# First batch of a fused attention and MLP kernel: last-chunk scores of chunks 2 to 4 computed once and transposed by DMA, diagonals of chunks 3 and 4 folded

## The chip, the cores and the metric

The kernel runs on one core of a Trainium2 chip. The metric is the device time of one execution in microseconds (us), as a median over several runs; lower is better. The core has a matrix engine (TensorE, PE in the profile), a vector engine (VectorE, DVE), a scalar engine with activation functions (ScalarE, ACT), a general engine (GpSimd, POOL) and a queue engine that issues transfers here (SyncE, SP). 16 DMA engines carry the transfers that SyncE, ScalarE and GpSimd issue.

## What is computed

There are 8 batches of 3008 rows. For each batch, with `z` of width 64, `v` and `u` of width 256:

```python
scores = (1.0 / S) * np.matmul(z, z.transpose(0, 2, 1))
attn = np.maximum(scores, 0.0) ** 2
x = u * np.matmul(attn, v)
```

and then, over all 24064 rows, a gated MLP with 2048 inner columns:

```python
h = x @ w_in
g = h * (1.0 / (1.0 + np.exp(-1.702 * h)))
out = g @ w_out
```

The score matrix is `z` times its own transpose, so it is symmetric: the block of keys a and queries b is the transpose of the block of keys b and queries a. The squared relu keeps that.

## The kernel before

**Tiles.** The 3008 rows of a batch are 24 blocks of 128 (`NJ`), the last one half full, or 6 chunks of 512 (`NCH`), the last one 448 wide. A *unit* `(i, jp)` is the score of the query chunk `i` against the key blocks `2*jp` and `2*jp + 1`, so a chunk of queries has 12 units. `scores` (lines 207 to 222) computes a unit with two matmuls of contraction 64, which sit in the two halves of TensorE's rows, into a PSUM tile `sc`; there are two such tiles. `square` (lines 224 to 254) then runs a relu on ScalarE (`rl`, line 231) and a square on VectorE (`a`, line 245). A unit with keys right of its own chunk is also transposed by a DMA, issued from SyncE (line 251), into half of a tile `tt`; the other chunk of the pair reads that tile in place of a unit of its own.

**Use.** `attend(b, i)` (lines 273 to 329) multiplies `v` by the squared scores for the queries of chunk `i`: one *step* for each key block `j`, in the order that the list `js` gives. `weights` (lines 256 to 270) says for a step where its scores lie: in a unit of chunk `i`, in a transposed tile, or, in later batches, in units of other chunks whose queries are already the last chunk. For chunks 0 and 1 of the first batch a step is one matmul over all 128 rows, in other cases two that share the array by halves of its rows.

**Two rules for the last chunk and the diagonal.** In batches 1 to 7, for chunks 0 to 4, the units `(i, 10)` and `(i, 11)` (last-chunk keys against queries of chunk `i`) are computed the other way round: as keys of chunk `i` against queries of chunk 5 (`turned`, line 212). Chunk 5 then reads them as they are, and chunk `i` reads their transposes, so chunk 5 has only two units of its own, `(5, 10)` and `(5, 11)`. Also in these batches the second of the two diagonal units is *folded* (line 204): only half of it is computed, and the other half comes by a DMA transpose (`ad`, line 238) from the first diagonal unit. In batch 0 neither is done: chunk 5 computes all its 12 units, and chunks 0 to 4 have plain units for its keys.

**Order of the work.** The order on each engine is the order in which the program is written, by hand. `pieces(b, i)` lists a chunk's units, `fill(b)` puts them in one queue, and the tables `SCHED0` (batch 0, lines 570 to 577) and `SCHED` say at which step of which chunk how many units are taken from the queue (`take`, line 581). So the scores of a chunk are computed in the steps of the chunk before it or its own. The loads of `u` come from GpSimd at steps given by `LOAD0`: that for chunk 3 at step 28 of chunk 1, that for chunk 4 at step 28 of chunk 2; each follows the turn of an earlier `u` tile on VectorE (line 194), whose buffer it takes. While batch 0 runs chunk 5, the first groups of the MLP (`up_group`) are set between its steps. SyncE's queue holds, in batch 0, the loads of `z` and `v`, then the transposes in the order of their units, with one load of `u` among them.

In batch 0 before, units are taken like this: all of chunk 0 and `(1, 2)`, `(1, 3)` by the end of chunk 0; in chunk 1 two units at each of the steps 0, 8, 15, 22, 30 and 38, which are the rest of chunk 1 and `(2, 4)` to `(2, 7)`; in chunk 2 `(2, 8)` to `(2, 11)` at steps 0, 3, 7 and 11, then the six of chunk 3; in chunk 3 the four of chunk 4 and two of chunk 5; in chunk 4 the other ten of chunk 5.

Of the kernel before, what the change touches and what calls it, by code (L numbers as in the profile page):

```python
# [15 lines left out]
def kernel(  # L16
# [20 lines left out]
    NJ = (S + P - 1) // P  # L37
# [3 lines left out]
    NCH = (S + CH - 1) // CH  # L41
    CB = CH // P
    NU = NJ // 2
# [38 lines left out]
    def post(last):  # L82

        sig = pool.nop()  # L84
        for m in last:
            tc.add_manual_dep(sig.ins, m.ins.name, SYNC, reason="row tiles of one bank")
        return sig

    def behind(sig, m):
        tc.add_manual_dep(m.ins, sig.ins.name, SYNC, reason="row tiles of one bank")  # L90
# [86 lines left out]
    def width(i):  # L177
        return CH if i < NCH - 1 else LAST
# [23 lines left out]


    def folded(b, i):
        return b > 0 and i < NCH - 1

    def scores(b, group):
        scs = []
        zt = ZT[b]
        for i, jp in group:  # L210
            sc = ps2.tile([P, 2, CH], F32, name="sc", tag="ps2")
            turned = b > 0 and i < NCH - 1 and jp >= NU - 2
            kp, qi = (2 * i + jp - (NU - 2), NCH - 1) if turned else (jp, i)
            m = CB // 2 if folded(b, i) and jp == 2 * i + 1 else CB
            for r in range(2):
                h = slice(r * DQK, (r + 1) * DQK)
                pe.matmul(  # L217
                    sc[:, r, :m * P], zt[h, 2 * kp + r, :], zt[h, (qi + 1) * CB - m:(qi + 1) * CB, :],
                    start=True, stop=True,
                )  # L220
            scs.append(sc)
        return [lambda u_=u_, sc=sc: square(b, *u_, sc) for u_, sc in zip(group, scs)]

    def square(b, i, jp, sc):
        rl = pw.tile([P, 2, CH], F16, name="rl", tag="rl", bufs=3)
        if folded(b, i) and jp == 2 * i + 1:
            rh = rl[:, :, :CH // 2]
            act.activation(rh, sc[:, :, :CH // 2], AF.Relu, scale=csc)
            dve.tensor_tensor(unit[b, i, jp][:, 1], rh, rh, ALU.mult)
            return  # L230
        act.activation(rl, sc, AF.Relu, scale=csc)  # L231
        if folded(b, i) and jp == 2 * i:
            a = pa.tile([P, CB, 2, P], F16, name="a", tag="a", bufs=21)
            unit[b, i, jp] = a
            r4 = rl.rearrange("p r (q c) -> p r q c", q=CB)
            dve.tensor_tensor(a.rearrange("p q r c -> p r q c"), r4, r4, ALU.mult)
            unit[b, i, jp + 1] = pa.tile([P, 2, 2, CH // 2], F16, name="ad", tag="a", bufs=21)
            sp.dma_start_transpose(
                unit[b, i, jp + 1][:, 0].rearrange("p g (r c) -> p (g r) c", c=P),
                a[:, CB // 2:].rearrange("p q r c -> p (q r c)"),  # L240
            )
            return
        a = pa.tile([P, 2, CH], F16, name="a", tag="a", bufs=21)
        unit[b, i, jp] = a
        dve.tensor_tensor(a, rl, rl, ALU.mult)  # L245
        cj = jp // 2
        if cj > i and (b or cj < NCH - 1):
            if (b, i, cj) not in TT:
                TT[b, i, cj] = pa.tile([P, CB, CB, P], F16, name="tt", tag="tt", bufs=14)
            k0 = 2 * (jp % 2)  # L250
            sp.dma_start_transpose(
                TT[b, i, cj][:, k0:k0 + 2].rearrange("p r g c -> p (r g) c"),
                a.rearrange("p r c -> p (r c)"),
            )

    def weights(b, i, j):

        cj, g = divmod(j, CB)
        n = NCH - 1
        if b == 0 and n in (i, cj):  # L260
            return unit[b, i, j // 2][:, j % 2, :width(i)]
        if i < n and cj == n:
            return TT[b, i, n][:, :, g, :]
        if folded(b, i) and cj == i:
            return unit[b, i, j // 2][:, :, g % 2, :]
        if i == n and cj < n:
            return unit[b, cj, NU - 2 + g // 2][:, g % 2, :LAST]
        if cj >= i:
            return unit[b, i, j // 2][:, j % 2, :width(i)]
        return TT[b, cj, i][:, :, g, :]  # L270


    def attend(b, i, both=False):


        n = width(i)
        js, cs = list(range(NJ - 1)), range(2)
        own = i * CB
        if b == 0 and i in (3, 4):
            js = js[own:-CB + 1] + js[:own] + js[-CB + 1:]  # L280
        elif b and i == NCH - 3:
            js = js[own:own + 2] + js[own + CB:-CB + 1] + js[:own] + js[own + 2:own + CB] + js[-CB + 1:]
        elif b and i < NCH - 2:
            js = js[own:own + 2] + js[own + CB:-CB + 1] + js[own + 2:own + CB] + js[:own] + js[-CB + 1:]
        half = [(0, TOP, NJ - 1), (1, LOW, NJ - 1)]
        if both:
            order = [[(c, FULL, j)] for j in js[:-CB] for c in cs] + [[(c, FULL, j)] for c in cs for j in js[-CB:]]
            order.insert(-CB, half)
        elif i == NCH - 1:
            order = [half] + [[(c, FULL, j)] for c in cs for j in js]  # L290
        else:
            order = [[(0, TOP, j), (1, LOW, j)] for j in js] + [half] + [[(1, TOP, j), (0, LOW, j)] for j in js]
        flat = [(k, m) for k, ms in enumerate(order) for m in ms]
        first = {c: next(m for m in flat if m[1][0] == c) for c in cs}
        final = {c: [m for m in flat if m[1][0] == c][-1] for c in cs}
        acc, turn = {}, NJ if order[-1][0][1] != FULL else -1

        def step(k):
            done = []
            for m in order[k]:  # L300
                c, h, j = m
                if (k, m) == first[c]:
                    acc[c] = ps1.tile([P, CH], F32, name="o", tag="ps1")
                ins = pe.matmul(  # L304
                    acc[c][:, :n], V16[b][h, j, c, :], weights(b, i, j)[h],
                    start=(k, m) == first[c], stop=(k, m) == final[c],
                )
                if k == turn:
                    behind(acc["sig"], ins)
                done.append(ins)  # L310
            if k == turn - 1:
                acc["sig"] = post(done)
            for c in cs:
                if k == final[c][0]:
                    gate(c)

        def gate(c):
            ut = UT[b, i][:, c].rearrange("p q t -> p (q t)")
            x = XT[b, i]
            if i < NCH - 1 or b % 2:  # L320
                dve.tensor_tensor(x[:, c, :n], acc[c][:, :n], ut[:, :n], ALU.mult)  # L321
            else:
                dve.tensor_tensor(x[:, c, :LFULL], acc[c][:, :LFULL], ut[:, :LFULL], ALU.mult)
                dve.tensor_tensor(XT[b + 1, i][:, c, LAST:], acc[c][:, LFULL:n], ut[:, LFULL:n], ALU.mult)

        XT[b, i] = XT.get((b, i)) or pa.tile([P, NCC, CH], F16, name="xt", tag="xt", bufs=6)
        if i == NCH - 1 and b % 2 == 0:
            XT[b + 1, i] = pa.tile([P, NCC, CH], F16, name="xo", tag="xo")
        return [lambda k=k: step(k) for k in range(len(order))]
# [202 lines left out]

    def pieces(b, i):

        lst = [(i, jp) for jp in range(2 * i if b or i < NCH - 1 else 0, NU)]
        if i == NCH - 1 or b == 0:
            return lst
        k = max(len(lst) - 6, 2)
        return lst[:k] + lst[-2:] + lst[k:-2]

    def split(lst, sizes):
        out_, k = [], 0
        for n in sizes:
            out_.append(lst[k:k + n])
            k += n
        assert k == len(lst)
        return out_

    TAIL = {1: {n: 1 for n in (3, 12, 44, 54)}, 2: {n: 1 for n in (4, 25, 34, 43)}}
    SCHED = {
# [16 lines left out]
    FIRST_ZT = {2: 2, 7: 3, 13: 4, 21: NCH - 1}  # L569
    SCHED0 = {  # L570
        0: {0: 1, 6: 2, 14: 2, 22: 2, 30: 2, 38: 2},
        1: {0: 2, 8: 2, 15: 2, 22: 2, 30: 2, 38: 2},
        2: {n: 1 for n in (0, 3, 7, 11, 30, 34, 38, 42)} | {NJ: 2},
        3: {n: 1 for n in (4, 9, 14, 19)} | {NJ: 2},
        4: {n: 1 for n in (0, 4, 8, 12, 16, 20, 31, 36)} | {NJ: 2},
        5: {},
    }

# [2 lines left out]
    def take(b, n):  # L581
        for post_ in scores(b, [queue.pop(0) for _ in range(n)]):
            post_()

    def fill(b):
        assert not queue
        queue.extend(u_ for i in range(NCH) for u_ in pieces(b, i))
# [20 lines left out]
    for b in range(B):  # L608
        nup = NCH * NFG
        sched, turn, load = (SCHED, TURN, LOAD) if b else (SCHED0, TURN0, LOAD0)  # L610
# [29 lines left out]
        for q in range(head, nup):  # L640
            if more and q in (head + 14, head + 20):
                k = int(q == head + 20)
# [46 lines left out]
```

## Time and profile before

| What | Value |
| --- | --- |
| median of 8 runs | 1206.49 us (1204.51 to 1209.34) |
| profiled execution | 1206.58 us, its span 1204.7 us |
| TensorE busy | 1191.9 us, 99% of the span |
| VectorE busy | 830.4 us, 69% |
| ScalarE busy | 770.3 us, 64% |
| attention of batch 0, chunks 1 to 4 | about 28 to 78 us of the span |
| transposes (tt) in batch 0 | 20 of 230 |

In the profile an engine's line shows its busy time, its share of the span and its instructions. A group is a line of the kernel with an engine, an operation and tiles (output<-input); then come its count, its busy time, the mean time of one in ns, and how long the engine stood idle before it and for whom. `sc` are scores, `rl` and `a` the relu and the square, `tt` the transposed tiles, `ad` a folded diagonal, `o` the attention output. SPq is SyncE's queue.

### The profile page before, as it was taken

The page shows a single profiled execution, that of the slowest core. Times are in us where ns is not written, and L with a number is a line of the kernel's source. Part 1 is how long each engine was busy: PE and PEld are TensorE (multiplying, and loading weights), DVE is VectorE, ACT ScalarE, POOL GpSimd, SP SyncE. Part 2 cuts the span into 40 slices and gives each one's busy share as a digit, 9 for nine tenths or more (in the row PEclk, how much of TensorE's full clock was granted, in tenths as well). Part 3 has the DMA queues.
Part 4 walks back from the last instruction along what each step waited for, and adds up shares of the span by engine and source line. Part 5 has one row for each costly group of instructions (what it writes and reads, how often), then busy time and mean ns, then how long its engine had stood idle before and what let it go on. Part 6 is the DMA issues. An engine that isn't in the chain of part 4 may idle for free.

```text
span 1204.7 us, 28259 instructions
## 1 busy us (share of the span) xinstructions
PE 1191.9 (99%) x11785; PEld 715.3 (59%) x11785; DVE 830.4 (69%) x1277; ACT 770.3 (64%) x903; POOL 307.1 (25%) x363
## 2 busy tenths in 40 slices
PE   8999999999999999999999999999999999999998
PEld 2446765467644675446765468554775547844577
DVE  6669955597546976469654696648966489564886
ACT  6777684576844768367683666736677376772764
POOL 4144300452004520044200451015510134101000
PEclk9999999999999999999999999999999999999999
DMA  9966389562994639854399443974459754496012
GB/s 231 163 107 125 122 157 161 91 153 74 171 161 87 150 93 169 156 82 137 94 187 144 80 137 98 193 132 77 137 120 189 126 84 149 113 182 115 1 37 71
DMA packets 366592, 152.33 MB, mean 126 GB/s; under 512 B 313312, under 2 KB 358496, under 8 KB 366464
## 3 DMA queue, kind: packets, MB, share of 16 engines
q1 hardware_dynamic: 330320, 114.08, 48.0%
q0 software_dynamic: 35456, 35.86, 14.9%
q8 instruction: 92, 1.51, 0.5%
q10 hardware_dynamic: 688, 0.59, 0.2%
q14 instruction: 36, 0.29, 0.1%
HBM read 60.29 MB, written 24.64 MB: 71 GB/s over the span
## 4 chain that ended last, share of the span: by engine, by line
PE 95%; DVE 2%; DMA 2%; ACT 1%; issue 0%; SPq 0%; ACTq 0%
PE o L304 38%; PE hg L345 26%; PE st L445 17%; PE yp L511 7%; PE sc L217 6%; DMA tt<-a 1%; DVE a L245 1%; ACT rl L231 0%; DVE gt L354 0%; DMA zf<-in_z_dram 0%; DVE zst L123 0%; ACT gf L353 0%; DVE s L416 0%; DVE s L418 0%; PE zp L129 0%
## 5 line engine op out<-in xcount | busy, mean ns | idle before, releaser
L353 ACT ACTIVATE gf<-hg 128x1024 f32<-128x1024 f32 (+1 forms) x384 | 385.8, 1007 | 165.0 <-PE hg L345 137.8
L231 ACT ACTIVATE rl<-sc 128x1024 f16<-128x1024 f32 x311 | 308.1, 1026 | 209.4 <-PE sc L217 207.4
L304 PEld LDWEIGHTS <-V 64*128 64x128 f16 (+1 forms) x4052 | 233.9, 94 | 252.6 <-issue 11.4
L345 PE MATMUL hg<-xt,W 128*128 128x512 f16 (+1 forms) x1408 | 354.5, 374 | 0.1
L354 DVE TENSOR_SCALAR gt<-gf 128x1024 f16<-128x1024 f32 (+1 forms) x384 | 275.5, 718 | 88.9 <-ACT gf L353 85.0
L245 DVE TENSOR_TENSOR a<-rl 128x1024 f16<-128x1024 f16 x276 | 192.0, 697 | 185.2 <-ACT rl L231 180.3
L304 PE MATMUL o<-a,V 64*128 64x512 f16 (+2 forms) x2010 | 317.2, 372 | 0.0
L187 POOL DMA_DIRECT2D uq<-in_u_dram x188 | 129.5, 696 | 511.1 <-PE sc L217 343.8
L304 PE MATMUL o<-tt,V 64*128 64x512 f16 (+1 forms) x1762 | 215.2, 376 | 2.2 <-DMA tt<-a 2.2
L345 PEld LDWEIGHTS <-W 128*128 128x128 f16 x1536 | 141.2, 98 | 117.4 <-issue 0.3
L445 PEld LDWEIGHTS <-gt 128*128 128x128 f16 x2176 | 132.4, 98 | 29.8 <-issue 1.1
L217 PE MATMUL sc<-ZT 64*128 64x512 f16 (+1 forms) x692 | 121.4, 367 | 1.8 <-DVE ZT L137 0.8
L445 PEld LDWEIGHTS <-s 128*128 128x128 f16 x1632 | 99.2, 98 | 20.7
L172 POOL CAST V<-vst 128x512 f16<-128x512 f32 x96 | 90.5, 981 | 64.8 <-DMA vst<-in_v_dram 51.0
L511 PE MATMUL yp<-W,gt 64*128 64x256 f16 x1664 | 103.9, 269 | 0.0
L511 PEld LDWEIGHTS <-gt 64*128 64x128 f16 x1664 | 80.4, 94 | 19.2 <-POOLq L84 4.1
L321 DVE TENSOR_TENSOR xt<-o,ut 128x512 f16<-128x512 f32 x80 | 51.5, 685 | 38.1 <-PE o L304 38.1
L445 PE MATMUL st<-WT,gt 128*128 128x128 f16 x1088 | 71.8, 219 | 0.9 <-ACT uP L455 0.9
L445 PE MATMUL st<-W,gt 128*128 128x128 f16 x1088 | 71.7, 219 | 0.0
L445 PE MATMUL st<-WT,s 128*128 128x128 f16 x1088 | 71.5, 219 | 0.0
L455 ACT ACTIVATE uP<-st 128x256 f32<-128x256 f32 x102 | 39.1, 383 | 39.6 <-DVE y L461 35.0
L217 PEld LDWEIGHTS <-ZT 64*128 64x128 f16 x692 | 37.5, 94 | 37.8 <-issue 7.1
(47 smaller groups left out, 628.6 us busy)
## 6 DMA issues: line engine op xcount, KB each, us to landing
vst<-in_v_dram SPq DMA_DIRECT2D x39, 512.0 KB, 5.1
uq<-in_u_dram POOLq DMA_DIRECT2D x156, 128.0 KB, 3.4
out_dram<-y SPq DMA_DIRECT2D x33, 512.0 KB, 3.8
tt<-a SPq DMA_TRANSPOSE x230, 3.5
uq<-in_u_dram POOLq DMA_DIRECT2D x32, 112.0 KB, 2.9
out_dram<-y POOLq DMA_DIRECT2D x7, 512.0 KB, 5.1
vst<-in_v_dram SPq DMA_DIRECT2D x8, 384.0 KB, 4.8
out_dram<-y POOLq DMA_DIRECT2D x7, 384.0 KB, 5.1
```

Source lines behind the costliest of these rows:

```text
L172: pool.tensor_copy(V16[b][:, n0:n0 + VB, k, :].rearrange("p n (q c) -> p n q c", c=QW), vst.rearrange("p n (q k c) -> p n q k c", k=NCC, c ...
L187: eng.dma_start(uq[k * QW:(k + 1) * QW, :n // QW].rearrange("t q k c -> t q (k c)"), src[:, :, cs])
L217: pe.matmul(sc[:, r, :m * P], zt[h, 2 * kp + r, :], zt[h, (qi + 1) * CB - m:(qi + 1) * CB, :], start=True, stop=True,)
L231: act.activation(rl, sc, AF.Relu, scale=csc)
L245: dve.tensor_tensor(a, rl, rl, ALU.mult)
L304: ins = pe.matmul(acc[c][:, :n], V16[b][h, j, c, :], weights(b, i, j)[h], start=(k, m) == first[c], stop=(k, m) == final[c],)
L321: dve.tensor_tensor(x[:, c, :n], acc[c][:, :n], ut[:, :n], ALU.mult)
L345: pe.matmul(hg[:, e, :n], W1[:, c, ff * P:(ff + 1) * P], XT[b, i][:, c, :n], start=(c == 0), stop=(c == NCC - 1),)
L353: act.activation(gf[:, :, :n], hg[:, :, :n], AF.Gelu_apprx_sigmoid, scale=1.0 / FSC)
L354: dve.tensor_scalar(g, gf[:, :, :n], FSC, None, ALU.mult)
L445: pe.matmul(bank[:, m, :], lhs()[:, f, m, :], right[:, ff, :], start=name in ("P1", "P2", "P5") and m == 0 and ff == 0, stop=ff == NFF // ...
L511: ins = pe.matmul(yp[s // per][:, s % per, :], GT[b, k, ff // CB][h, ff % CB, s * P:(s + 1) * P], W2[h, ff, :], start=new, stop=n == last[ ...
```

## The change

In batch 0, chunks 2, 3 and 4 follow the rule of the later batches for the last chunk (`turned` is now a function), and chunks 3 and 4 fold their second diagonal unit. Chunk 5 of batch 0 keeps the units `(5, 0)` to `(5, 3)`, for the keys of chunks 0 and 1, and `(5, 10)`, `(5, 11)`; six units are no longer computed. Six units more are transposed by DMA, and two half diagonals. In a chunk whose last-chunk units are turned, these two are now taken first. `SCHED0` takes units at other steps: chunk 1 at steps 0, 7, 14, 21, 28 and 34 (two each) and 40 (one), which now end with `(2, 10)` and `(2, 11)` at step 28, `(2, 4)`, `(2, 5)` at 34 and `(2, 6)` at 40; chunk 2 at 0, 4, 8, 24 (two), 28, 33, 38 and 43. The order of steps changes too: chunk 2 reads blocks 0 to 11, then 20 to 22, then 12 to 19; chunk 3 takes the order that the later batches have; chunk 4 takes the natural order.

```diff
     def folded(b, i):
-        return b > 0 and i < NCH - 1
+
+        return i < NCH - 1 and (b > 0 or i > 2)
+
+    def turned(b, i):
+
+        return i < NCH - 1 and (b > 0 or i > 1)
...
-            turned = b > 0 and i < NCH - 1 and jp >= NU - 2
-            kp, qi = (2 * i + jp - (NU - 2), NCH - 1) if turned else (jp, i)
+            turn = turned(b, i) and jp >= NU - 2
+            kp, qi = (2 * i + jp - (NU - 2), NCH - 1) if turn else (jp, i)
...
-        if cj > i and (b or cj < NCH - 1):
+        if cj > i and (turned(b, i) or cj < NCH - 1):
...
-        if b == 0 and n in (i, cj):
+        if n in (i, cj) and not turned(b, min(i, cj)):
             return unit[b, i, j // 2][:, j % 2, :width(i)]
...
-        if b == 0 and i in (3, 4):
-            js = js[own:-CB + 1] + js[:own] + js[-CB + 1:]
-        elif b and i == NCH - 3:
+        if b == 0 and i == 2:
+            js = js[:own + CB] + js[-CB + 1:] + js[own + CB:-CB + 1]
+        elif i == NCH - 3:
             js = js[own:own + 2] + js[own + CB:-CB + 1] + js[:own] + js[own + 2:own + CB] + js[-CB + 1:]
...
-        lst = [(i, jp) for jp in range(2 * i if b or i < NCH - 1 else 0, NU)]
-        if i == NCH - 1 or b == 0:
-            return lst
+        lst = [(i, jp) for jp in range(2 * i, NU)]
+        if i == NCH - 1:
+            return [(i, jp) for jp in range(2 * i) if not turned(b, jp // 2)] + lst
+        if b == 0:
+            return lst[-2:] + lst[:-2] if turned(b, i) else lst
...
-        1: {0: 2, 8: 2, 15: 2, 22: 2, 30: 2, 38: 2},
-        2: {n: 1 for n in (0, 3, 7, 11, 30, 34, 38, 42)} | {NJ: 2},
-        3: {n: 1 for n in (4, 9, 14, 19)} | {NJ: 2},
-        4: {n: 1 for n in (0, 4, 8, 12, 16, 20, 31, 36)} | {NJ: 2},
+        1: {0: 2, 7: 2, 14: 2, 21: 2, 28: 2, 34: 2, 40: 1},
+        2: {n: 1 for n in (0, 4, 8, 28, 33, 38, 43)} | {NJ: 2},
+        3: {n: 1 for n in (4, 9, 14)} | {NJ: 2},
+        4: {n: 1 for n in (4, 12, 34)} | {NJ: 2},
         5: {},
```

An unused helper, `split`, is also removed.

More of the change, by code (lines that the diff above doesn't have):

```diff
@@ L533, in pieces @@
     def pieces(b, i):
-        lst = [(i, jp) for jp in range(2 * i if b or i < NCH - 1 else 0, NU)]
-        if i == NCH - 1 or b == 0:
-            return lst
+        lst = [(i, jp) for jp in range(2 * i, NU)]
[3 more added lines that the diff above has]
+            return lst[-2:] + lst[:-2] if turned(b, i) else lst
         k = max(len(lst) - 6, 2)
         return lst[:k] + lst[-2:] + lst[k:-2]
[L541 to L547, printed above, removed]
     TAIL = {1: {n: 1 for n in (3, 12, 44, 54)}, 2: {n: 1 for n in (4, 25, 34, 43)}}
```

## The prediction

> **What bounds the kernel now.** I read the page first, then the chain that ended last, then TensorE's order in the first 80 us, then the DMA queues of that stretch.
>
> ```profile
> PE 1191.9 (99%) x11785; PEld 715.3 (59%) x11785; DVE 830.4 (69%) x1277; ACT 770.3 (64%) x903; POOL 307.1 (25%) x363
> ...
> PE 95%; DVE 2%; DMA 2%; ACT 1%; issue 0%; SPq 0%; ACTq 0%
> ...
> L304 PE MATMUL o<-tt,V 64*128 64x512 f16 (+1 forms) x1762 | 215.2, 376 | 2.2 <-DMA tt<-a 2.2
> ```
>
> The chain is TensorE for 95%. So a matmul that goes is worth its full slot, and a wait of TensorE costs its full length: it has no slack in which to make it up. The last line shows the one wait of attention matmuls that the whole run knows: 2.2 us for transposed blocks (tt) that had not landed. The change puts more such blocks into the first batch, so I ask when they land.
>
> TensorE around the border of chunks 1 and 2 of the first batch, in order of time (start, length, line, tiles):
>
> ```profile
> 36.84 0.60 PE L217 MATMUL sc<-ZT 64*128 64x512 f16 x4
> 37.37 1.90 PE L304 MATMUL o<-a,V 128*128 128x512 f16 x8
> 39.21 0.60 PE L217 MATMUL sc<-ZT 64*128 64x512 f16 x4
> 39.74 2.33 PE L304 MATMUL o<-a,V 128*128 128x512 f16 x10
> 42.01 0.39 PE L217 MATMUL sc<-ZT 64*128 64x512 f16 x2
> 42.23 0.81 PE L304 MATMUL o<-tt,V 64*128 64x512 f16 x6
> ```
>
> These give the slots. A unit of scores or a pair of row tiles takes 0.216 us (42.01 to 42.23). In chunk 1, which works with full 128-row tiles, a visit to scores costs 0.21 us more than its matmuls: 36.84 to 39.21 is 2.37 us for 2 units and 8 matmuls, ten slots, 2.16 us.
>
> The SyncE queue in the same stretch, where the transposes are issued, and two of them alone; then, for each of those two, the time from issue to landing; then VectorE's squares of units (1,8) and (1,9), and GpSimd:
>
> ```profile
> 31.78 19.03 SPq L251 DMA_TRANSPOSE tt<-a  x9
> ...
> 42.53 2.83 SPq L251 DMA_TRANSPOSE tt<-a  x1
> ...
> 45.45 1.39 SPq L251 DMA_TRANSPOSE tt<-a  x1
> ```
> ```profile
> DMA to landing us min/median/max: 7.3/7.3/7.3
> ...
> DMA to landing us min/median/max: 5.1/5.1/5.1
> ```
> ```profile
> 33.75 0.69 DVE L245 TENSOR_TENSOR a<-rl 128x1024 f16<-128x1024 f16 x1 [0.55 <-ACT rl L231]
> 34.66 0.69 DVE L245 TENSOR_TENSOR a<-rl 128x1024 f16<-128x1024 f16 x1 [0.22 <-ACT rl L231]
> ...
> 39.01 2.57 POOL L187 DMA_DIRECT2D uq<-in_u_dram  x4 [9.34 <-DVE ut L194]
> ```
>
> Nine transposes stand back to back over 19.0 us, 2.1 us each, though the shortest issue in this queue is 1.2 us. Their sources wait for the queue: (1,8) and (1,9) are squared by 34.4 and 35.4, but are issued at 39.2 and 40.6. The queue is behind by 5 us, and while the fourth u load of GpSimd (39.0 on) shares the DMA engines, a transpose takes 5 to 7 us to land. Before, nobody minds: the two issued at 42.5 and 45.4 are (2,6) and (2,7), whose block is first read in chunk 3, at about 58 us.
>
> **The change part by part.**
>
> *Score work that goes.* Chunk 5 drops 6 of its 12 units: 6 x 0.216 = 1.30 us of TensorE. The second diagonal unit of chunks 3 and 4 is half as wide: 2 x 0.108 = 0.22 us. Sum 1.52 us. ScalarE and VectorE lose 6 x 1.03 and 6 x 0.69 us and two halves; they end nothing here (64% and 69% busy), so that is worth nothing by itself.
>
> *Score work that moves.* Chunk 1 now has seven visits to scores (steps 0, 7, 14, 21, 28, 34, 40) with 13 units, not six with 12. The unit is only moved; the visit adds 0.21. Visits stand 6 or 7 steps apart, 1.94 to 2.15 us, and ScalarE needs 1.94 us for a pair of units with two score buffers, so a later unit waits for its buffer: I take 0.4 us in all (0.1 to 0.7; the one visit before that comes 7 steps after another loses 0.05).
>
> *The two transposes in front.* Units (2,10) and (2,11) are now scored at step 28 of chunk 1. Before, the visit at step 30 began at 36.84 with as many units behind it, so this one begins near 36.4. ScalarE is done with the pair by 38.8, VectorE, with the turn of u ahead of it, by about 39.8. On SyncE the same 12 transposes of chunks 0 and 1 and the u load stand ahead of them as before, so they are issued in the very places that (2,6) and (2,7) had: 42.5 and 45.4. With those rows' times they land at 42.53 + 7.3 = 49.8 and 45.45 + 5.1 = 50.6.
>
> *Who waits.* In chunk 2 the new order reads blocks 0 to 11, and then 20 to 22, which is the transposed block of these two units; both halves are needed at once. Chunk 2 begins at 42.01 + 0.22 + 0.21 + 0.4 = 42.8. Twelve steps and three units (steps 0, 4, 8) are 15 x 0.216 = 3.24 us, so the block is wanted at 46.1 and is there at 50.6: TensorE stands for 4.5 us. Queued behind on TensorE are 35 steps of chunk 2 and the visits to scores of chunk 3, so ScalarE, VectorE and the later transposes start later too; nothing runs ahead meanwhile. Bounds: if the two land as the quickest row of this stretch (issue 1.3, landing 3.2 us), 42.5 + 1.3 + 3.2 = 47.0, a stand of 0.9 us; with the longest landing among the first batch's twenty (8.6 us; their median is 5.9), 54.0, 7.9 us. I take 4.5, because the rows are those of the same queue places behind the same loads.
>
> *The clock after the stand.* The only long gap of TensorE before is that at 13 us. By stretches (length; busy time of PE, PEld, DVE, ACT, POOL; granted clock; DMA):
>
> ```profile
> 13.30:15.30 2.00, 0.00 (x0) 0.00 (x0) 2.00 (x4) 0.39 (x1) 2.00 (x3) 1.00 1.20 279
> 15.40:18.70 3.30, 3.07 (x12) 1.01 (x13) 1.80 (x5) 1.46 (x2) 3.30 (x7) 0.50 1.14 223
> ```
>
> After a gap of 2.4 us the clock is halved for some 3.3 us. A gap of 4.5 us will do the same. How much of the slow stretch falls inside the gap is open: none costs 1.7 us, all of it 0. I take 1.2, as part of it should lie in so long a gap.
>
> The Trainium skill ("TensorE: Matmul & The Clock Gate", section "Why this matters for your kernels") allows gaps up to about 3 us before the clock falls; here 2.4 us were enough, so the row decides that even a shorter stand would cost clock. By that page's window of 3.4 us at half rate the term would be 1.7 and the sum 0.5 us higher.
>
> *The other transposes.* Six more come: the pairs (3,10),(3,11) and (4,10),(4,11) and two folded diagonals. The pair of chunk 4 has most of a chunk, 12 us, of time. In chunk 3 the folded diagonal is read after 18 steps and three visits, 4.5 us into the chunk; its score stands at step 28 of chunk 2, 19 steps and some units earlier, about 9.5 us before its use. Square and score take 2.4 us, the transpose 2.5 (median of ad) to 6.5 us with two others ahead and a u load beside it: between 2 us early and 1.5 us late. I take 0.2. A folded square costs the same as a plain one (0.692 against 0.697 us in the next batch).
>
> The Trainium skill ("DMA: Bandwidth & Descriptors", section "Latency and other measured facts") gives 261 GB/s for a DMA transpose, an estimate of 1.0 us for one of these 256 KB. Behind the transpose issued at 40.55, which takes 6.9 us to land, the pair would by that be there at 49.5, and the sum 1.1 us lower; the rows of this stretch, where u loads share the engines, say 50.6.
>
> *Sum.* -1.52 + 0.21 + 0.4 + 4.5 + 1.2 + 0.2 = +5.0 us. The profiled execution took 1206.58 us (span 1204.7), practically the median of 1206.49, so the forecast is 1211.5 us. From the second batch on, order and loads are as before; I carry no term for them.
>
> **The rivals.**
>
> A. The block is in time, or nearly: the transposes are served faster than in the rows, because SyncE's backlog isn't bound by the u load. For it: two transposes of this queue are issued in 1.3 and land in 3.2 to 3.3 us (at 36.5 and 37.8 us). It decides from a landing before about 47.5. Then -1.52 + 0.6 + 0.9 at most, without loss of clock: 1205.7 to 1206.6, not slower. Against it: (1,9), one place ahead and unchanged, lands only at 47.5. Chance 0.09.
>
> B. A middle: landing near 48.5 to 49, a stand of 2.5 us, little of the slow clock: 1208 to 1209.3. Chance 0.08.
>
> C. The queue stays behind, and the folded diagonal or the pair of chunk 3 makes a second stand of 1.5 to 3 us, or the first is near its upper bound, with a full slow stretch: 1214 to 1217. For it: the u load at step 28 of chunk 2 again meets three new transposes. Against: SyncE has the first stand to drain. Chance 0.13.
>
> That the dropped work is worth nothing isn't a rival of weight: it comes off TensorE. But 1.5 us is less than 2.4 us, the 0.2% that a measurement of this kernel can tell from no change, so without any new wait it would still count as the same.
>
> **How the numbers follow.** Forecast 0.70, with its own range 1209.8 to 1213.3. To leave out no more than 2 in 10 the range goes down to most of B and up into C: 1208.4 to 1215.0. Slower by over 0.2% (above 1208.9): 0.70 + 0.13 + half of B = 0.87. Within 0.2%: A and the rest of B, 0.11. Faster by over 0.2%: 0.02, since the dropped work cannot reach it.
>
> **What would show it.** TensorE gets a wait for a tt block of 4 to 5 us, near 46 us, in chunk 2; the granted clock shows a half-speed stretch there; SyncE issues the new pair near 42.5 and 45.4 us, with landings near 50; scores lose 12 matmuls (692 to 680) and the chunk 5 stretch is shorter. It is wrong if the pair is issued well before 42 us, if it lands within 4 us, or if the wait is there and the clock stays at 1.00 throughout, which would take 1.2 us off.

## The result and the profile after

The changed kernel takes 1212.18 us (median of 22 runs, 1207.66 to 1215.08), the kernel before 1206.77 us (59 runs, 1204.15 to 1210.32). The ratio is 1.0043, with a 95% interval of 1.0035 to 1.0050: slower by 5.4 us, against 5.0 us in the forecast. Here and below, medians and ratios are those of the fast runs (experiments 4, 8 and 10 had one slow run each), and a ratio compares all runs of both sides, so it is not the quotient of the two medians. The profiled execution took 1212.95 us, with a span of 1211.2 us against 1204.7 us.

The page of the changed kernel, the lines that answer to those of before (busy time of each engine, the chain that ended last, and the groups of the scores and of the attention on transposed tiles):

```profile
PE 1193.3 (99%) x11773; PEld 717.5 (59%) x11773; DVE 825.7 (68%) x1271; ACT 763.4 (63%) x897; POOL 307.2 (25%) x363
...
PE 94%; DMA 2%; DVE 1%; ACT 1%; issue 1%; SPq 0%; ACTq 0%
...
L309 PE MATMUL o<-tt,V 64*128 64x512 f16 (+1 forms) x1804 | 221.5, 377 | 7.9 <-DMA tt<-a 7.6
...
L222 PE MATMUL sc<-ZT 64*128 64x512 f16 (+1 forms) x680 | 119.7, 367 | 1.4 <-DVE ZT L137 0.8
```

TensorE has 12 matmuls fewer (11773 for 11785; the scores are now 680), and yet 1.4 us more of busy time, as part of its matmuls ran at half clock (below). Its wait for transposed tiles grew from 2.2 to 7.6 us. The order of TensorE's work shows where:

```profile
41.75 0.39 PE L222 MATMUL sc<-ZT 64*128 64x512 f16 x2
...
43.92 0.38 PE L222 MATMUL sc<-ZT 64*128 64x512 f16 x2
44.13 1.03 PE L309 MATMUL o<-a,V 64*128 64x512 f16 x8
50.08 1.46 PE L309 MATMUL o<-tt,V 64*128 64x512 f16 x6 [4.92 <-DMA tt<-a]
51.34 3.62 PE L309 MATMUL o<-a,V 64*128 64x512 f16 x16
```

Chunk 2 begins at 41.75 us; after 15 slots, at 45.16 us, TensorE stands for 4.92 us for a `tt` tile. The 16 matmuls that follow, eight slots of 0.216 us, take 3.62 us, about twice the time of eight slots. SyncE's queue, and the time to landing of the two transposes that TensorE waits for:

```profile
17.36 42.87 SPq L256 DMA_TRANSPOSE tt<-a  x20
60.33 1.22 SPq L243 DMA_TRANSPOSE ad<-a  x1
```
```profile
L256 SPq DMA_TRANSPOSE tt<-a x2: 2193/2638/3084, 42.5 to 45.6; - x2
...
DMA to landing us min/median/max: 4.4/5.6/6.9
```

SyncE is at work on twenty transposes for 42.9 us, with one wait of 4.1 us among them, at 53.4 us, for a square; up to the pair they follow one another directly. The pair (2,10), (2,11) is squared by 38.1 and 38.7, issued at 42.5 and 45.6, and landed at 49.3 and 50.0. The stretches of the clock (length; busy time of PE, PEld, DVE, ACT, POOL; granted clock; DMA share, GB/s):

```profile
45.30:48.60 3.30, 0.00 (x0) 0.00 (x0) 0.69 (x1) 0.07 (x1) 0.00 (x0) 1.00 1.27 182
48.70:52.00 3.30, 1.92 (x10) 0.72 (x12) 0.00 (x0) 0.00 (x0) 0.00 (x0) 0.51 1.01 202
52.10:55.40 3.30, 3.30 (x18) 1.18 (x16) 0.00 (x0) 0.00 (x0) 0.00 (x0) 0.50 1.26 154
55.50:58.90 3.40, 3.36 (x32) 1.60 (x30) 1.81 (x3) 3.10 (x4) 0.00 (x0) 0.99 0.02 4
```

The clock record has half speed from 48.75 for 6.83 us, two stretches of 3.41 us. TensorE works from 50.08 to 55.58 of it at half rate: its 14 slots up to 55.81 take 5.73 us in place of 3.02, a loss of 2.7 us.

**The balance of this trace.** The first MLP matmul, the mark of chunk 5, comes at 78.76 us before and at 84.64 us after, 5.88 later:

```profile
78.76 1.03 PE L345 MATMUL hg<-xt,W 128*128 128x512 f16 x4
```
```profile
84.64 1.03 PE L350 MATMUL hg<-xt,W 128*128 128x512 f16 x4
```

Chunk 2 begins 0.26 us earlier (41.75 for 42.01). From there on: the stand 4.92, the clock 2.7, and eight units fewer between this point and chunk 5 (52 score matmuls before, 34 whole and 4 half ones after; six dropped, two halves, one moved ahead into chunk 1), -1.73. Together 5.63; 0.25 us are not accounted for. From chunk 5 to the last matmul the two traces differ by 0.6 us (1122.08 and 1122.64).

### The profile page after: what moved, and what is told of

It reads as the page before. It is cut to its first block, busy times and chain, and to the rows that moved or that the text cites. A ratio compares the mean times of both kernels' runs of the same rounds, so it can differ in the third digit from the quotient of the medians.

```text
span 1211.2 us, 28237 instructions
## 1 busy us (share of the span) xinstructions
PE 1193.3 (99%) x11773; PEld 717.5 (59%) x11773; DVE 825.7 (68%) x1271; ACT 763.4 (63%) x897; POOL 307.2 (25%) x363
## 4 chain that ended last, share of the span: by engine, by line
PE 94%; DMA 2%; DVE 1%; ACT 1%; issue 1%; SPq 0%; ACTq 0%
PE o L309 37%; PE hg L350 26%; PE st L450 17%; PE yp L516 8%; PE sc L222 6%; DMA tt<-a 2%; ACT rl L236 1%; DVE a L250 0%; DMA zf<-in_z_dram 0%; DVE gt L359 0%; ACT gf L358 0%; DVE zst L123 0%; DVE s L421 0%; PE zp L129 0%; DVE s L423 0%
## 5 line engine op out<-in xcount | busy, mean ns | idle before, releaser
L236 ACT ACTIVATE rl<-sc 128x1024 f16<-128x1024 f32 x303 | 300.2, 1026 | 221.2 <-PE sc L222 219.5
L250 DVE TENSOR_TENSOR a<-rl 128x1024 f16<-128x1024 f16 x266 | 184.3, 694 | 194.8 <-ACT rl L236 191.4
L309 PE MATMUL o<-a,V 64*128 64x512 f16 (+2 forms) x1952 | 312.6, 374 | 0.0
L309 PE MATMUL o<-tt,V 64*128 64x512 f16 (+1 forms) x1804 | 221.5, 377 | 7.9 <-DMA tt<-a 7.6
```

What stands on the lines that cost most here:

```text
L309: ins = pe.matmul(acc[c][:, :n], V16[b][h, j, c, :], weights(b, i, j)[h], start=(k, m) == first[c], stop=(k, m) == final[c],)
```

## The experiments

The question was which part costs, whether the late pair is a matter of SyncE's queue, of the `u` load beside it or of the place where the block is read, and what the slow clock is worth. Each run stands against runs of the kernel before on the same chip (medians 1206.68 to 1206.82 us). The diffs are against the changed kernel.

**1. Read the late block at the end of chunk 2.**

```diff
-        if b == 0 and i == 2:
-            js = js[:own + CB] + js[-CB + 1:] + js[own + CB:-CB + 1]
-        elif i == NCH - 3:
+        if i == NCH - 3:
```

> The changed kernel, but chunk 2 of the first batch reads its blocks in natural order, so the turned pair's block is read 8 steps (1.7 us) later. Theory (the pair's transposes are late for that read): the wait shrinks from 4.9 to about 3.2 us, landing unchanged near 50 us; 1.5 to 3 us faster than the changed kernel, about 2 to 4 us slower than before. Rival (the loss comes from the six more transposes and the folds of chunks 3 and 4, wherever the block is read): same time as the changed kernel, 5.4 us slower than before.

Measured: 1209.74 us, ratio 1.0031 (1.0016 to 1.0046). TensorE's order:

```profile
43.80 2.11 PE L307 MATMUL o<-a,V 64*128 64x512 f16 x18
49.08 1.89 PE L307 MATMUL o<-tt,V 64*128 64x512 f16 x8 [3.17 <-DMA tt<-a]
50.76 1.06 PE L222 MATMUL sc<-ZT 64*128 64x512 f16 x4
```

With eight more steps ahead of the block, 1.7 us of cover, the stand is 3.17 us, and the clock is halved for one stretch. Less seems to be lost, though the interval overlaps with that of the changed kernel (1.0035 to 1.0050). The pair is still late, though its block is now the last of the chunk's first pass: the place of the reading is not the whole of it.

**2. Leave chunk 2 as it was.**

```diff
     def turned(b, i):
-        return i < NCH - 1 and (b > 0 or i > 1)
+        return i < NCH - 1 and (b > 0 or i > 2)
...
-        4: {n: 1 for n in (4, 12, 34)} | {NJ: 2},
+        4: {n: 1 for n in (4, 12, 16, 20, 34)} | {NJ: 2},
```

(and chunk 2 in its natural order, as in experiment 1)

> The changed kernel with chunk 2 as before: its last-chunk units are not turned, chunk 5 computes two more units (eight), natural order of blocks in chunk 2. Chunks 3 and 4 stay turned and folded. Theory: no wait of TensorE in chunk 2, no half-speed clock there; -0.86 us for four units, -0.22 for the folds, +0.2 for the seventh visit and +0.3 for score buffers: 0.6 us under before, measured as the same. Rival (chunks 3 and 4 carry the loss): at least 3 us slower than before.

Measured: 1207.13 us, ratio 1.0007 (0.9993 to 1.0020): no difference from before. So all of the loss that a median shows hangs on turning chunk 2. A gain of the other edits can't be seen: the 0.6 us that was expected lies inside the interval, and so does nothing at all. The traced execution is one of the longer ones (1211.0 us) and shows why:

```profile
62.73 0.61 PE L307 MATMUL o<-ad,V 64*128 64x512 f16 x4 [2.87 <-DMA ad<-a]
```

The folded diagonal of chunk 3 lands too late in this execution, and the clock is halved after it, too. This is the mechanism of rival C of the prediction, without chunk 2's stand.

**3. Keep TensorE busy in the wait.** Twenty matmuls on a tile of zeros go in front of the block's reading; their result is not used.

```diff
+                if b == 0 and (i, n) == (2, 3 * CB):
+                    warm_up(20)
```

> The changed kernel with 20 matmuls on zeros (20 x 0.216 = 4.3 us, their result unread) put on TensorE just where it stands for the turned pair in chunk 2, so that the wait is as long but TensorE is busy in most of it. Theory (the wait also costs clock): the half-speed stretch after it goes, the remaining wait is about 0.5 us, and the kernel is 1.0 to 2.7 us faster than the changed one, 3 to 4.5 us slower than before. Rival (the wait costs its length only, or the clock goes by other things): within 0.5 us of the changed kernel.

Measured: 1210.5 us, ratio 1.005 (1.003 to 1.007), with runs from 1206.26 to 1218.14. The traced execution is the longest of them. In chunk 2 it does what it should: a wait of 0.7 us and a granted clock of 1.00. But chunk 4 has a stand of 5.0 us for its folded diagonal, with a half-speed stretch:

```profile
PE o L309 <- DMA ad<-a: 5.2, 2, 5.0
```
```profile
45.00:50.00 5.00, 5.00 (x32) 2.10 (x29) 1.53 (x3) 1.52 (x2) 0.00 (x0) 1.00 1.38 138
78.00:81.30 3.30, 0.00 (x0) 0.00 (x0) 0.00 (x0) 0.00 (x0) 0.00 (x0) 1.00 1.11 134
81.40:84.80 3.40, 3.28 (x16) 1.18 (x18) 0.00 (x0) 0.08 (x1) 0.00 (x0) 0.50 0.55 108
```

Seven of the twelve runs, with a mean granted clock of 0.998 or more, take 1206.26 to 1211.05 us; the five others, at 0.997, take 1215.73 to 1218.14 us. By time this decides nothing on the clock. It shows that the transposes of chunks 3 and 4 have no slack that could be relied on.

**4. Score the pair fourteen steps earlier,** at step 14 of chunk 1.

```diff
+        if b == 0 and i == 1:
+            return lst[:4] + [(2, NU - 2), (2, NU - 1)] + lst[4:]
+        if b == 0 and i == 2:
+            return lst[:-2]
```

> The changed kernel with the turned pair (2,10), (2,11) scored at step 14 of chunk 1, ahead of (1,6) to (1,11), instead of step 28; so its two transposes stand four places earlier in SyncE's queue. Nothing else differs. Theory (place in the queue is the cause): issue near 36 and 37 us, landing by 39 to 43 us, wanted at 45: no wait, no half-speed stretch; 0.7 us under before, measured as the same or just faster. Rival (the DMA engines are short of rate, so any place moves the wait to another block or chunk): a wait of over 2 us for another tt or ad tile, 3 us or more slower than before.

Measured: 1209.95 us, ratio 1.0029 (1.0011 to 1.0046). The pair is issued at 34.8 and 36.1, lands at 38.1 and 39.5, and nobody waits for it. The stand is now elsewhere:

```profile
58.96 1.04 PE L309 MATMUL o<-tt,V 64*128 64x512 f16 x8
64.80 1.04 PE L309 MATMUL o<-ad,V 64*128 64x512 f16 x4 [4.79 <-DMA ad<-a]
```
```profile
39.06 2.57 POOL L187 DMA_DIRECT2D uq<-in_u_dram  x4 [9.12 <-DVE ut L194]
53.40 2.57 POOL L187 DMA_DIRECT2D uq<-in_u_dram  x4 [11.77 <-PE sc L222]
```

TensorE no longer stands in chunk 2, so it reaches chunk 3 earlier, and there the folded diagonal is late: behind the pair (3,10), (3,11), whose transposes are issued at 54.5 and 56.1 beside the next `u` load (53.4 on) and take 9.0 and 8.2 us to land, it is issued only at 59.6 and lands at 64.8. The half-speed stretch follows. In the first trace of the changed kernel this diagonal is issued at 60.3, landed at 66.1 and wanted only at 66.34, since the stand in chunk 2 had come before: the first stand is the cover of the second.

**5 to 7. The `u` loads at other steps; the clock.** Experiment 5 sets the loads for chunks 4 and 5 later, 6 adds the twenty matmuls of experiment 3 to it, 7 was to set that for chunk 3 later as well.

```diff
-    LOAD0 = {(i, n): i + 2 for i, n in TURN0 if i + 2 < NCH}
+    LOAD0 = {(0, 38): 2, (1, NJ + 4): 3, (3, 40): 4, (4, 10): 5}
```

(in experiment 7 with `(2, 13): 3` in place of `(1, NJ + 4): 3`)

> The changed kernel with the loads of u for chunks 4 and 5 of the first batch set later (step 40 of chunk 3, step 10 of chunk 4), away from the folded diagonals' transposes; the load for chunk 3 stays at step 28 of chunk 1. Theory: the pair's wait in chunk 2 stays (4 to 5 us, landing near 50 us) with its half-speed stretch, no wait for a folded diagonal in any execution: about 5 us slower than before, with less scatter than the changed kernel with the pair early had. Rival (the wait in chunk 2 has nothing to do with the pair's queue place and goes with any change of loads): under 2 us slower than before.

> The kernel with the u loads of chunks 4 and 5 later, and 20 matmuls on zeros (4.3 us, result unread) where TensorE stands in chunk 2. Theory (the stand also costs clock): no half-speed stretch after 45 us, a wait of under 1 us left, 1.0 to 2.7 us faster than the same kernel without the fill. Rival (the clock term is nothing): within 0.5 us of it.

> As the kernel with the later u loads of chunks 4 and 5, and the u load of chunk 3 too is set later: from step 28 of chunk 1 to step 13 of chunk 2, behind the read of the pair's block. Theory (the u load, sharing the DMA engines, makes the transposes slow): the pair is issued near 41 and 42 us and lands by 46; a wait of 0 to 1 us, no half-speed stretch, 0 to 0.9 us under before, measured as the same. Rival (SyncE's transposes alone fill the DMA engines): landing at 48 us or later, wait of over 3 us, 4 us or more slower than before.

Measured: 1213.93 us (1.0065, 1.0053 to 1.0077), 1211.4 us (1.0038, 1.0024 to 1.0051) and 1210.06 us (1.0033, 1.0020 to 1.0046). The stands in chunk 2 are 5.0, 1.4 and 1.2 us.

In experiment 7 the edit did nothing. GpSimd issues this load when its buffer is free and does not wait for TensorE's step; each engine has the same instructions in the same order as in experiment 5, and the load stands where it stood:

```profile
39.01 2.57 POOL L187 DMA_DIRECT2D uq<-in_u_dram  x4 [9.12 <-DVE ut L194]
```

So 5 and 7 are one program, measured twice in one job, and yet 3.9 us apart. Their runs don't overlap (1212.85 to 1215.68 and 1209.36 to 1212.18 us). In 5 the pair is issued at 40.8 and 43.7 and lands at 49.5 and 50.3; in 7 it is issued at 39.3 and 40.6 and lands at 44.8 and 47.5. The stand goes with it, 5.0 and 1.2 us, and so does the clock: half speed for two stretches in 5, for none in 7.

For the price of the clock, the time from TensorE's first matmul behind the stand to chunk 5 is compared, which is the same work. In 5 it is 34.54 us (50.38 to 84.92), and in the first trace of the changed kernel 34.56 (50.08 to 84.64); in 6, where zeros fill the wait and the clock stays at 1.00, it is 31.86 (52.14 to 84.00), and in 7 it is 31.86 as well (47.57 to 79.43). Two half-speed stretches after the stand therefore cost 2.7 us, more than twice the forecast's term. The medians agree, 6 being 2.5 us under 5, but they alone would not show it, as 5 and 7 differ by more.

```profile
52.45:55.80 3.35, 3.35 (x18) 1.18 (x16) 0.00 (x0) 0.00 (x0) 0.00 (x0) 0.50 0.98 122
```
```profile
52.20:56.00 3.80, 3.80 (x36) 1.70 (x37) 0.00 (x0) 0.84 (x1) 0.00 (x0) 1.00 1.09 215
```

The first line is from experiment 5, the second from 6: 18 matmuls in 3.35 us, and 36 in 3.80 us.

**8. Both: the pair early, and the `u` loads later.** The edits of experiments 4 and 7 together.

> All three u loads later and the turned pair scored at step 14 of chunk 1. Theory: no wait for tt or ad in the first batch, clock 1.00 from 20 us on; the dropped work alone is left, 0.5 to 1.2 us under before. Rival (the folded diagonal of chunk 3 or 4 is late by its own place, not by the u load): a wait of 2 us or more for ad, 2 us or more slower than before.

Measured: 1218.99 us, ratio 1.0096 (1.0063 to 1.0130), runs up to 1223.85. The trace, that of the longest of these, first TensorE, then the three transposes issued at 60.9 to 64.5 us with their landing, then GpSimd:

```profile
87.00 1.04 PE L309 MATMUL o<-ad,V 64*128 64x512 f16 x4 [15.21 <-DMA ad<-a]
```
```profile
L256 SPq DMA_TRANSPOSE tt<-a x3: 1352/2043/2566, 60.9 to 64.5; - x3
...
DMA to landing us min/median/max: 4.2/9.2/20.6
```
```profile
62.85 1.08 POOL L387 DMA_DIRECT2D W<-in_moe_w_in_dram  x2 [0.29 <-issue]
63.90 2.63 POOL L187 DMA_DIRECT2D uq<-in_u_dram  x4
66.49 0.59 POOL L387 DMA_DIRECT2D W<-in_moe_w_in_dram  x1
67.02 1.31 POOL L187 DMA_DIRECT2D uq<-in_u_dram  x2
```

The `u` loads now meet the weights of the MLP, all issued by GpSimd from 62.9 us on. Transposes issued beside them take up to 20.6 us to land, and TensorE stands for 15.2 us in front of chunk 4's folded diagonal. The idea was wrong: together with the early pair, the loads were only moved into a worse place. (In experiments 5 to 7 they meet the weights as well, but begin only once the last diagonal's transpose has been issued, at 63.2 to 68.7 us, and TensorE has no stand for a diagonal.)

**9. Hold back the `u` load for chunk 3, this time with a wait.** GpSimd waits for step 12 of chunk 2 before it goes on, and so the load starts after the pair.

```diff
+            if (b, i, k) == (0, 2, 3 * CB):
+                post(done)
...
-    LOAD0 = {(i, n): i + 2 for i, n in TURN0 if i + 2 < NCH}
+    LOAD0 = {(2, 13) if i == 1 else (i, n): i + 2 for i, n in TURN0 if i + 2 < NCH}
```

> The changed kernel in which GpSimd waits, ahead of the u load for chunk 3, for TensorE's 13th step of chunk 2, which is the first that reads the pair's block; so that load cannot share the DMA engines with the pair. Unlike the edit of the program's order alone, this does hold the load back. Theory (the u load makes the transposes slow to land): the pair is issued near 39 to 42 us and lands by 44 to 46.5; TensorE waits 0 to 1.3 us and the clock stays; what the load then does to the folded diagonal of chunk 3 (a wait of 0 to 5 us) is open, so 0 to 5 us slower than before. Rival (SyncE's transposes fill the DMA engines by themselves): landing at 48 us or later and a wait of over 3 us as before.

Measured: 1207.96 us, ratio 1.0016 (1.0001 to 1.0030). GpSimd, then the pair and its two neighbours in SyncE's queue, then TensorE's waits in chunks 2 to 4:

```profile
47.36 2.57 POOL L187 DMA_DIRECT2D uq<-in_u_dram  x4 [17.62 <-DVE a L250]
53.53 2.57 POOL L187 DMA_DIRECT2D uq<-in_u_dram  x4 [3.60 <-DVE ut L194]
```
```profile
L256 SPq DMA_TRANSPOSE tt<-a x4: 1274/1286/1292, 39.8 to 43.9; - x4
...
DMA to landing us min/median/max: 3.2/3.9/4.3
```
```profile
PE o L309 <- DMA ad<-a: 1.7, 1, 1.7
PE o L309 <- DMA tt<-a: 0.2, 1, 0.2
```

With the load out of the way the pair is issued at 41.2 and 42.6, takes 1.3 us each to issue, and lands 4.3 and 3.8 us later; in the two traces of the changed kernel issue takes 1.4 to 3.1 us and landing 4.4 to 7.7. The pair is there at 46.4, the stand is 0.2 us, and after 20 us the clock stays at 1.00 in batch 0. The slow landing goes with the load: the next transpose issued beside it, at 48.3 us, takes 8.4 us to land. Against the changed kernel, which took 1211.01 us in the same job (experiment 10), 3.1 us come back; by time alone that would not be enough, with 3.9 us between experiments 5 and 7, but the interval also ends below that of the changed kernel's first measurement (1.0035 to 1.0050). So it is the `u` load beside them that makes these transposes slow to land. The Trainium skill ("DMA: Bandwidth & Descriptors", section "Issuing engines are not separate DMA queues") says that transfers issued from several engines run on the same 16 DMA engines and interleave, and these rows agree. Of the stands in chunks 2 to 4 that of chunk 3's folded diagonal is left, 1.7 us; it now meets both loads. The traced execution is one of the longer ones (1211.11 us), and 3.3 us of its excess over the trace of before lie behind the mark of chunk 5, where at 1060.6 us TensorE stands for 2.66 us for another transposed tile and a half-speed stretch follows.

**10. The changed kernel once more.**

> The changed kernel itself once more, for a second trace of it, since two programs with the same instructions on every engine gave waits of 5.0 and 1.4 us. Theory (the landing of the pair scatters by some 2 to 3 us from execution to execution): a wait for the pair between 1 and 5 us, the clock halved only where it is over 2 us, and the span follows the wait; 4 to 7 us slower than before in the median. Rival (the changed kernel always waits 4.9 us): the same wait within 0.3 us.

Measured: 1211.01 us, ratio 1.0040 (1.0023 to 1.0057). The pair is issued at 39.7 and 41.2 and lands at 47.0 and 48.9:

```profile
45.32 1.03 PE L309 MATMUL o<-a,V 64*128 64x512 f16 x8
48.96 0.82 PE L309 MATMUL o<-tt,V 64*128 64x512 f16 x6 [2.61 <-DMA tt<-a]
```

The stand is 2.61 us here and 4.92 us in the first trace, and the clock stays at 1.00 after it. In chunk 4 there is a second stand, 1.4 us for a folded diagonal. Chunk 5 begins at 82.39 us in this execution and at 84.64 us in the first one. So the first trace shows one outcome of the changed kernel and not the only one.

**11 and 12. Chunk 2 alone, twice.** Only chunk 2 is turned; there is no fold in batch 0, and chunks 3 and 4 have the order and the units of before.

```diff
-        return i < NCH - 1 and (b > 0 or i > 2)
+        return i < NCH - 1 and b > 0
...
-        return i < NCH - 1 and (b > 0 or i > 1)
+        return i < NCH - 1 and (b > 0 or i == 2)
...
+        elif b == 0 and i in (3, 4):
+            js = js[own:-CB + 1] + js[:own] + js[-CB + 1:]
...
-        4: {n: 1 for n in (4, 12, 34)} | {NJ: 2},
+        4: {n: 1 for n in (4, 8, 12, 16, 20, 31, 36)} | {NJ: 2},
```

> One part of the change alone: in the first batch only chunk 2 is turned; chunks 3 and 4 are as before, with no fold and no transpose for the last chunk, and chunk 5 computes ten units. Theory (chunk 2's pair carries the loss): a wait of 1 to 5 us for its block and most of the loss, 2 to 6 us slower than before. Rival (the folds and turns of chunks 3 and 4 carry it): no more than 1 us slower than before.

> Chunk 2 alone turned, once more: its median of five was 9.9 us over before, above the theory's 2 to 6, while its profiled execution (3.6 us over) showed a wait of 1.8 us for the pair. Theory (the landing of the pair scatters, and a long wait also halves the clock): over more executions 3 to 6 us slower than before, and a trace of a slow one shows a wait of 4 us or more for the block of chunk 2 with a half-speed stretch. Rival (turning chunk 2 alone makes a second wait elsewhere): a wait of over 2 us for another tt block in the first batch.

Measured: 1216.67 us (1.0076, 1.0051 to 1.0101; runs from 1210.05 to 1218.91) and, in another job, 1212.45 us (1.0048, 1.0036 to 1.0060). Chunk 2 alone loses at least as much as the whole change. In the second trace:

```profile
43.74 1.03 PE L311 MATMUL o<-a,V 64*128 64x512 f16 x8
48.60 1.46 PE L311 MATMUL o<-tt,V 64*128 64x512 f16 x6 [3.83 <-DMA tt<-a]
```

The only stand of batch 0 for a transposed tile is that of chunk 2, 3.83 us, with one half-speed stretch after it (48.14 to 51.55). From TensorE's first matmul behind the stand to chunk 5 it is 34.52 us here and 33.08 us in the first of the two traces, where the clock stays at 1.00: one stretch costs 1.4 us. Why the first of these two measurements is 4 us above the second is open: its traced execution is its fastest (1210.05 us, a stand of 1.7 us), and none of its long ones was traced.

No kernel of the set is faster than the kernel before. The nearest are experiments 2 (1.0007) and 9 (1.0016).

## Why the prediction was right, and where its terms were off

The time and the sign were right, and the first trace shows the mechanism as it was forecast: a pair that is late behind SyncE's queue and a `u` load, a stand of TensorE in chunk 2, and a slow clock after it. Against the prediction's own profiled execution the forecast was +5.0 us; the median rose by 5.4 us, the traced execution by 6.4 us. In the trace of experiment 10, though, two of the prediction's own signs of being wrong are there: the first of the pair is issued at 39.7 us, well before 42, and TensorE waits while the clock stays at 1.00. The steps one by one:

- **Score work that goes, -1.52.** The matmuls went as stated (692 to 680, and two diagonals by half). The balance of the first trace closes to 0.25 us with this term. But its gain can't be seen in a median: experiment 2 keeps part of it (four dropped units and two halves, 1.08 us) and can't be told from before.
- **Score work that moves, +0.21 and +0.4.** In experiment 10 chunk 2 begins at 42.93 us, against 42.8 in the forecast and 42.01 before. This agrees to 0.1 us. In the first trace it begins at 41.75, 1.2 us earlier than in experiment 10 with the same program. There an early half-speed stretch lies at 7.79 to 11.21 us and not, as before, at 15.34 to 18.76; the two go together, but whether the place of that stretch makes the 1.2 us was not tested.
- **The transposes in front.** Forecast: issued at 42.5 and 45.4, landed by 50.6. First trace: 42.5, 45.6 and 50.0. The premise, that the pair takes the very places of (2,6) and (2,7), held in this execution. (The rows have 14 transposes of chunks 0 and 1 ahead of it and not 12, and the load at 39.0 is GpSimd's third; neither changes the sum.) Over nine traces with the same order up to there and the pair at its place (the changed kernel's two, experiments 1, 3, 5, 6, 7, 11 and 12) the later landing is at 47.5 to 52.1 us, with a median of 49.0. So the rows of one profiled execution gave one place in the later half of a spread of 4.6 us, which the forecast took for the place itself.
- **Who waits, +4.5.** 4.92 us in the first trace, for the reason given there: chunk 2 is early by 1.0 us, the pair by 0.6 us. Over the six of these traces that read the block at the same place, with nothing put in the wait (without experiments 1, 3 and 6), the stand is 1.2 to 5.0 us; the block lands at 47.5 to 50.3 us and is wanted at 44.8 to 46.4. The forecast's bounds, 0.9 and 7.9, held.
- **The clock, +1.2 (0 to 1.7).** This is the term that was mis-sized: 2.7 us where it fell in full, outside the bounds. The forecast took one stretch, part of it inside the gap. In the first trace 1.3 us did lie inside the gap, but the stretch in which TensorE resumed was followed by a second one. Where TensorE resumed within 0.5 us of the stretch's start (experiments 1 and 12) it was the only one, which is 1.4 us by experiments 11 and 12 and inside the bounds. In other executions the term is nothing at all (experiments 7 and 10, stands of 1.2 and 2.6 us), so the reading that a gap of 2.4 us is enough to halve the clock doesn't hold by length alone. How often the term falls can be read from the mean granted clock of each run: of the 22 runs of the first measurement 18 are at 0.996 or 0.997 (an estimate from 0.997: some 7 us at half speed, two stretches), and the four at 0.999 are the four fastest, 1207.66 to 1210.43 us. The runs of the kernel before in the experiments' jobs are all at 0.998 to 1.000.
- **The other transposes, +0.2.** In the first trace the folded diagonal of chunk 3 lands 0.2 us before its use and costs nothing. In experiment 10 that of chunk 4, for which the forecast has no term, costs 1.4 us. The bounds for chunk 3 (2 us early to 1.5 late) held in the two traces of the changed kernel; in experiments 2 and 4, without the stand in chunk 2, its diagonal costs 2.9 and 4.8 us with a slow stretch. The forecast had said of rival C that SyncE would have the first stand to drain in, and experiment 4, where the stand is gone, shows this cover.
- **From the second batch on, no term.** The first trace has 0.6 us. But from chunk 5 to the end the fourteen traces take from 1121.7 to 1125.3 us, so this part is not as still as the missing term implies: TensorE's waits of over 0.2 us there add up to 3.0 to 5.7 us, most of them for transposed tiles.

Of the rivals, A (in time) is what experiment 9 has to make by hand: only with the load held back does the pair land clearly before the 47.5 us that it asked for, at 46.4. Its premise was half right. SyncE's place does not hang on the load alone (over the nine traces the first of the pair is issued at 39.3 to 43.7 us beside the load, and at 41.2 without it); the time to landing does, and that is enough to make it late in each of the nine. B (a middle) is what experiment 10's execution shows in chunk 2, a stand of 2.6 us with no slow clock. C (a second stand) is there in part of the executions. The forecast treated these three as cases of which one would be the kernel's. They are outcomes of the same program, from one execution or one measurement to the next, and the median of 1212.18 us lies among them, so that the closeness to 1211.5 us owes something to luck, to terms that cancel: a clock term too small by 1.5 us where it falls, and a stand that is shorter in four of the six traces.

## What to carry to other kernels

Before a transposed tile replaces a recomputed one, look at the issue queue and at the other transfers of that stretch. What is saved here was 0.2 us of a matmul for each unit; a transpose that waits its turn in a full queue, beside a load that slows it, cost TensorE up to 5 us and then the clock. If a stand is taken away, read the next place with little slack in the same trace, since the stand may have been its cover; and a load that shall come later needs a wait, not another place in the program. Durations of one trace are one draw: where landings scatter by 4.6 us, give a term its spread.

## What the runs showed of the hardware

**Half-speed stretches lie on a grid.** In every trace with more than one their starts are whole multiples of 3.413 us apart. In the first trace of the changed kernel 7.79 and 48.75: 40.96 us, 12.0 times 3.413. In experiment 4 16.79 and 64.58, 14.0 times; in experiment 8 15.85 and 73.88, 17.0 times; in experiment 9 15.62 and 1063.51, 307.0 times. Where the grid lies against the start differs between executions. So the same gap can cost clock in one execution and not in another; by these rows, what decides is how TensorE was busy in one whole cell of the grid. The cell before a slow stretch, in the kernel before (first line, 11.90 to 15.30), and two full cells of experiment 10 with its stand of 2.61 us:

```profile
11.90:15.30 3.40, 1.38 (x8) 0.41 (x5) 3.40 (x5) 1.79 (x3) 3.40 (x4) 1.00 1.16 307
```
```profile
43.90:47.20 3.30, 2.45 (x24) 0.88 (x20) 2.26 (x4) 2.53 (x3) 0.00 (x0) 1.00 1.45 139
47.35:50.65 3.30, 1.69 (x16) 0.80 (x18) 0.00 (x0) 0.00 (x0) 0.00 (x0) 1.00 1.06 199
```

A cell that was busy for 1.38 of 3.4 us was followed by half speed, though the gap that it holds most of was 2.36 us; cells with 2.45 and 1.69 of 3.3 us were not, since the border of the grid, at 47.33, split the longer gap of 2.61 us. In the first trace after the change the stand filled one cell (half speed follows), and the next, at half speed, was busy for 1.92 of 3.3 us, and half speed went on. This reading of the rows was made afterwards; no kernel was run to test it. The Trainium skill ("TensorE: Matmul & The Clock Gate", section "What's actually happening") states a free-running window of 3413 ns, and the multiples agree with it.

**A transpose is slowed for long by a load of GpSimd.** Without one beside it, it was issued in 1.3 us and landed in 3.2 to 4.3 us (experiment 9); in the 8 us after the `u` load for chunk 3 had begun (four transfers of 128 KB), in 1.4 to 4.2 us and 4.4 to 7.8 us (the changed kernel's two traces); beside `u` and weight loads it took up to 20.6 us to land (experiment 8).

**One program, two outcomes.** Chunk 5 of experiments 5 and 7, the same instructions in the same order, begins at 84.92 and 79.43 us, and their medians differ by 3.9 us. All runs of 5 lie above all of 7, so it is not only scatter from one execution to the next. Why SyncE's queue moves faster in one than in the other was not found.
